# Eleven closing stores of a decode-layer gradient kernel, issued by SyncE instead of GpSimd

## The chip, the cores and the metric

The kernel runs on one core of one Trainium2 chip. A core has five engines with a queue of instructions each: TensorE (PE, with its weight loads as PEld), VectorE (DVE), ScalarE (ACT), GpSimd (POOL) and SyncE (SP, which computes nothing). Data between HBM and the on-chip memory is moved by 16 DMA engines; a transfer is issued by one of the engine queues, and its landing is told by a semaphore. The metric is the device time of one execution in microseconds (us); the times of several executions are given by their median. In the profile, times count from the first instruction, and the span is the time from the first to the last one.

## What is computed

The kernel computes one decode step of a transformer layer (attention over a window of cached keys and values, then a gated feed-forward stage, both with layer norms modulated by a condition vector `c`), and all its gradients for a given `grad_out`. The forward part of the reference, cut to what matters here:

```python
# B = S = 1, D = 1024, 32 query heads, 4 key/value heads, head size 128, cache 65536, window W = 4096
mod = (silu(c) @ w_mod).reshape(1, 6, 1, -1)              # sa, ca, ga, sb, cb, gb
h = layernorm(x) * (1 + ca) + sa
x = x + ga * attention(h, k_cache[..., -W:, :], v_cache[..., -W:, :], wq, wo)
h = layernorm(x) * (1 + cb) + sb
x = x + gb * ((sigmoid(h @ w_gate) * (h @ w_up)) @ w_down)
return x
# outputs: x, and by jax.vjp the gradients of x, k_cache, v_cache, wq, wo, w_gate, w_up, w_down, c, w_mod
```

There is a single token, so every weight gradient is an outer product of two vectors: the row of the gradient of `wq` that belongs to input `j` is `h1[j]` times the gradient of `q`. The gradients of the two caches are zero outside the window (120 MB of zeros in all) and dense in the 4096 positions inside it.

## The kernel before, in words

Only the memory traffic is large: 60.30 MB are read and 185.60 MB written. The schedule is written out by hand: each engine executes its instructions in the order in which the program text records them, and a framework adds the semaphore waits (for data, for buffers that are to be overwritten, and for the DMA semaphores themselves). DMAs issued by GpSimd use eight semaphores in turn, those issued by SyncE and ScalarE eight others; a DMA whose semaphore is still held by an earlier one waits for that one's landing.

GpSimd issues nearly all transfers: the caches, the weights, the zero stores of the cache gradients (`zero`, L160 to L169, placed all over the program so that the DMA engines have work at all times), and nearly all dense results. SyncE issues the first loads of `w_mod`, the loads and stores of `w_down` and its gradient in the feed-forward stage (`load_wd` L852, `store_wd` L855), two late loads (L1120) and three small rows of results (`col_to_row_out`, L251).

The big on-chip buffer is `arena`, cut by hand: `ar(off, size)` is a piece of `size` KB per partition. Buffers are used again as soon as their last use is over. In the closing stage these matter:

- `sec(j)` (L1122) forms columns 2048 to 6143 of the gradient of `w_mod` for block `j` on VectorE, and stores 1 MB from `sec_t[j]`. `sec_t[7]` lies at 56, 8 KB long.
- `dV(g)` and `dK(g)` (through `grad_kv`, L1153) form the dense part of a cache gradient: 32 small matmuls per head, eight evictions `L1162` (ScalarE) or `L206` (VectorE; for dK the two take turns), and one store of 1 MB at L1167, from `kv_home`.
- `dwq_tile(j)` (L1172) is an outer product on VectorE (`outer_dve`, recorded as L206) and a store of 1 MB (L1174), from `dwq_t[j]`.
- `s2(j)` (L1176) forms columns 0 to 2047 of the gradient of `w_mod` on VectorE (also L206) and stores 512 KB (L1178), from `s2_t[j]`. `s2_t[3]` lies at 56, so `s2(3)` has to wait for the landing of `sec(7)`'s store.

The last part of the program is `dK(0)`, `dwq_tile(4)`, `s2(0)`, `s2(1)`, `dK(1)`, and then the eleven steps `dwq_tile(5)`, `s2(2)`, `s2(3)`, `dK(2)`, `dwq_tile(6)`, `s2(4)`, `s2(5)`, `dK(3)`, `dwq_tile(7)`, `s2(6)`, `s2(7)`. At that place all zero stores have been issued. The closing line of the kernel (L1330 in the profile of the kernel before) holds what the framework adds: SyncE waits for every semaphore of the program, each engine executes a DRAIN and reports to GpSimd, GpSimd waits for the other four, clears semaphores and releases them, in two rounds.

Of the kernel before, what the change touches and what calls it, by code (L numbers as in the profile page):

```python
# [19 lines left out]
D = 1024  # L20
# [14 lines left out]
SCALE = DH ** -0.5  # L35
# [23 lines left out]
def kernel(  # L59
# [26 lines left out]
    nc = tc.nc  # L86
# [13 lines left out]
    def ar(off, size):  # L100
        return arena[:, int(off * KIB):int((off + size) * KIB)]
# [79 lines left out]
    def new_ps(name="ps"):  # L181
        p, tag = next_pool()
        return p.tile([P, 512], FP32, name=name, tag=tag)
# [17 lines left out]
    def cp(out, a):  # L201
        return nc.vector.tensor_copy(out=out, in_=a)  # L202

    def ts(out, a, s1, op0, s2=None, op1=None):
        if op1 is None:
            return nc.vector.tensor_scalar(out=out, in0=a, scalar1=s1, scalar2=None, op0=op0)  # L206
        return nc.vector.tensor_scalar(out=out, in0=a, scalar1=s1, scalar2=s2, op0=op0, op1=op1)
# [35 lines left out]
    def outer_dve(out, col, b):  # L243
        return ts(out, b, col, ALU.mult)
# [65 lines left out]
    dwq_view = out_4.rearrange("(j p) n -> p j n", p=P)  # L310
    dwm_view = out_10.rearrange("(j p) n -> p j n", p=P)
# [797 lines left out]
    dS = ar(168, 8)  # L1109
# [3 lines left out]
    kv_home = [ar(o, 8) for o in (184, 64, 72, 80, 96, 104, 112, 120)]  # L1113
    dwq_t = [ar(o, 8) for o in (88, 40, 152, 0, 8, 16, 32, 48)]
    s2_t = [ar(o, 4) for o in (148, 24, 28, 56, 60, 184, 188, 64)]
# [26 lines left out]
    def make_hd(src, name):  # L1142
        tp = new_tp("tp_hd")
        for g in range(G):
            nc.tensor.transpose(tp[32 * g:32 * g + 32, 0:P], src(g), ident_bf[:, :], tile_position=(0, 32 * g))
        hd = late.pop()
        cp(hd, tp[:, 0:P])
        return hd

    def kv_out(og, g):  # L1150
        return og[0, g, SKW:, :].rearrange("(p t) d -> p (t d)", t=KT)

    def grad_kv(rows, hd, og, scale, g, dst, engs):  # L1153
        for tb in range(KT // 4):
            ps = new_ps("ps_kv")
            for t4 in range(4):
                t_ = tb * 4 + t4
                nc.tensor.matmul(ps[:, t4 * DH:(t4 + 1) * DH], lhsT=rows[32 * g:32 * g + HG, t_ * P:(t_ + 1) * P],  # L1158
                                 rhs=hd[32 * g:32 * g + HG, :], start=True, stop=True, tile_position=(32 * g, 0))
            o = dst[:, tb * 512:(tb + 1) * 512]  # L1160
            if engs[tb % len(engs)] == "A":
                nc.scalar.activation(out=o, in_=ps[:, :], func=ACT.Copy, scale=float(scale))  # L1162
            elif scale == 1.0:
                cp(o, ps[:, :])
            else:
                ts(o, ps[:, :], float(scale), ALU.mult)
        nc.gpsimd.dma_start(out=kv_out(og, g), in_=dst)  # L1167

    dV = lambda g, engs: grad_kv(P_b2, DO_hd, out_3, 1.0, g, kv_home[g], engs)
    dK = lambda g, engs: grad_kv(dS, Q_hd, out_2, SCALE, g, kv_home[4 + g], engs)  # L1170

    def dwq_tile(j):  # L1172
        outer_dve(dwq_t[j], h1[:, j:j + 1], dq_b)
        nc.gpsimd.dma_start(out=dwq_view[:, j, :], in_=dwq_t[j])  # L1174

    def s2(j):  # L1176
        outer_dve(s2_t[j], cs_col[:, j:j + 1], dmod_b2)
        nc.gpsimd.dma_start(out=dwm_view[:, j, 0:2 * D], in_=s2_t[j])  # L1178

    zero(Z_END[0])  # L1180
    do_ps = new_ps("do_ps")[:, 0:HQ]
# [32 lines left out]
    Q_hd = make_hd(lambda g: q_col2[:, HG * g:HG * g + 32], "Q_hd")  # L1214
# [36 lines left out]
    dV(0, "A")  # L1251
    sec(4)
    dwq_tile(0)
    dV(1, "A")
    zero(Z_END[3])
    sec(5)
    dwq_tile(1)
    dV(2, "A")
    sec(6)
    dwq_tile(2)  # L1260
    bcast(dmod_bf[:, 0:16], 16, dmod_b2, "A")
    dcs01 = matvec_T(lambda jb, nb: w01_T[:, nb, jb * P:(jb + 1) * P], dh1_hl, "dcs01")
# [24 lines left out]
    dK(0, "AV")  # L1287
    dwq_tile(4)
    s2(0)
    s2(1)  # L1290
    dK(1, "AV")
    dwq_tile(5)
    s2(2)
    s2(3)
    dK(2, "AV")
    dwq_tile(6)
    s2(4)
    s2(5)
    dK(3, "AV")
    dwq_tile(7)  # L1300
    s2(6)
    s2(7)
    keep[0] = 0
    zero(len(zleft))
    assert not zleft and not narrow and not jobs and not bq
# [29 lines left out]
```

## Time and profile before

| | us |
|---|---|
| median of 3 runs | 601.98 |
| lowest and highest of them | 601.69, 602.49 |
| the profiled execution | 600.56 |
| its span | 598.5 |
| busy in it: PE, PEld, DVE | 408.8, 275.9, 336.6 |
| busy in it: ACT, POOL | 266.2, 166.8 |

The span was filled with 412 GB/s on average. How to read what follows: the page cuts the span into 40 equal slices of 15 us and gives for each the mean busy share of the 16 DMA engines in tenths, and what they moved in GB/s. The stretches are the same sums for windows that the reader chooses; a DMA share somewhat above 1 comes from packets that overlap on an engine. The timeline gives each instruction's start, its duration, its engine and line, what it writes and reads, and in brackets how long the engine had been idle before it and what ended that. A GpSimd DMA instruction shows in it only with the time of its issue; its landing is found with the DMA's own line. A line such as "L1330 POOLq DRAIN x3: 46/93/16344" gives the shortest, median and longest duration in ns, and then the first and last start in us.

### The profile page before, as it was taken

The page shows a single profiled execution, that of the slowest core. Times are in us where ns is not written, and L with a number is a line of the kernel's source. Part 1 is how long each engine was busy: PE and PEld are TensorE (multiplying, and loading weights), DVE is VectorE, ACT ScalarE, POOL GpSimd, SP SyncE. Part 2 cuts the span into 40 slices and gives each one's busy share as a digit, 9 for nine tenths or more (in the row PEclk, how much of TensorE's full clock was granted, in tenths as well). Part 3 has the DMA queues.
Part 4 walks back from the last instruction along what each step waited for, and adds up shares of the span by engine and source line. Part 5 has one row for each costly group of instructions (what it writes and reads, how often), then busy time and mean ns, then how long its engine had stood idle before and what let it go on. Part 6 is the DMA issues. An engine that isn't in the chain of part 4 may idle for free.

```text
span 598.5 us, 11039 instructions
## 1 busy us (share of the span) xinstructions
PE 408.8 (68%) x4587; PEld 275.9 (46%) x4612; DVE 336.6 (56%) x641; ACT 266.2 (44%) x408; POOL 166.8 (28%) x264
## 2 busy tenths in 40 slices
PE   3997688999999989999984435544445096765300
PEld 3995334334344545546653434434434066555300
DVE  3653499999511010160007598795796887768530
ACT  2489514567212014213225565673664746873200
POOL 3113123222222212222221233342423363122330
PEclk9999699999999999999995555555555586755555
DMA  8999999999999999999999999999999999999996
GB/s 348 420 417 421 414 427 413 427 423 425 428 419 425 423 427 424 422 424 423 423 397 412 420 387 413 406 398 414 406 404 412 420 422 412 421 424 426 424 416 279
DMA packets 45026, 246.63 MB, mean 412 GB/s; under 512 B 5085, under 2 KB 5085, under 8 KB 24544
## 3 DMA queue, kind: packets, MB, share of 16 engines
q0 software_dynamic: 39120, 225.99, 98.2%
q1 hardware_dynamic: 5808, 19.93, 9.9%
q8 instruction: 36, 0.59, 0.4%
q14 instruction: 14, 0.11, 0.0%
q10 hardware_dynamic: 48, 0.01, 0.0%
HBM read 60.30 MB, written 185.60 MB: 411 GB/s over the span
## 4 chain that ended last, share of the span: by engine, by line
PE 43%; DMA 26%; DVE 17%; ACT 6%; issue 5%; POOL 0%; ACTq 0%; POOLq 0%; SPq 0%; DVEq 0%
PE b_ps L692 17%; DMA out_dram<-arena 15%; DMA arena<-in_B_w_gate_dram 7%; PE n_ps L637 6%; DVE arena L206 4%; DVE arena L193 4%; DVE arena L210 3%; DVE junk L210 3%; PE t_ps L599 2%; DMA arena<-in_B_w_down_dram 2%; PE tp_side L837 2%; ACT arena L838 2%; PE tp_wq L454 2%; PE w_ps L395 2%; PE tp_k L435 1%
## 5 line engine op out<-in xcount | busy, mean ns | idle before, releaser
L692 PE MATMUL b_ps<-arena 128*128 128x512 bf16 x494 | 113.4, 379 | 1.0 <-issue 0.2
L169 POOL DMA_DIRECT2D out_dram<-zeros x114 | 62.3, 548 | 179.7 <-DMA out_dram<-zeros 56.6
L837 PE MATMUL tp_side<-ident_bf,arena 128*128 128x128 bf16 x432 | 51.7, 300 | 48.8 <-ACT arena L838 41.9
L193 DVE TENSOR_TENSOR arena<-arena 128x2048 bf16<-128x2048 bf16 x64 | 76.5, 1223 | 2.3 <-PE n_ps L637 0.3
L692 PEld LDWEIGHTS <-arena 128*128 128x128 bf16 x512 | 48.7, 98 | 55.9 <-issue 2.9
L838 ACT COPY arena<-tp_side 128x1024 bf16<-128x1024 bf16 x54 | 54.0, 1012 | 41.7 <-PE tp_side L837 40.8
L210 DVE CUSTOM_DVE_ANT_0 arena<-arena,scr 128x1024 bf16<-128x1024 bf16 x56 | 66.2, 1220 | 9.8 <-ACT scr L991 9.8
L637 PE MATMUL n_ps<-arena 128*128 128x512 bf16 x249 | 65.1, 378 | 6.9 <-DVE arena L193 5.0
L837 PEld LDWEIGHTS <-arena 128*128 128x128 bf16 x432 | 43.4, 139 | 53.8 <-issue 53.4
L241 ACT ACTIVATE arena<-scr,h 128x1024 bf16<-128x1024 bf16 x35 | 40.1, 1148 | 9.6 <-DVE dh2acc L210 7.8
L637 PEld LDWEIGHTS <-arena 128*128 128x128 bf16 x256 | 24.6, 97 | 41.6 <-issue 16.2
L202 DVE CAST arena<-b_ps 128x512 bf16<-128x512 f32 x6 | 4.1, 691 | 61.6 <-PE b_ps L692 61.6
L1162 ACT ACTIVATE arena<-ps_kv 128x512 bf16<-128x512 f32 x48 | 26.1, 681 | 27.9 <-PE ps_kv L1158 27.5
L210 DVE CUSTOM_DVE_ANT_0 junk<-arena,b1k 128x1024 bf16<-128x1024 bf16 x28 | 34.2, 1222 | 6.1 <-DMA arena<-in_B_w_down_dram 5.7
L601 ACT CAST arena<-t_ps 128x512 bf16<-128x512 f32 x56 | 30.1, 589 | 12.1 <-PE t_ps L599 12.1
L1158 PE MATMUL ps_kv<-junk,arena 8*128 8x128 bf16 x256 | 27.1, 304 | 11.1 <-DVE arena L206 9.8
L869 POOL DMA_DIRECT2D out_dram<-arena x28 | 21.4, 768 | 39.7 <-ACT arena L241 29.8
L1158 PEld LDWEIGHTS <-arena 8*128 8x128 bf16 x256 | 25.2, 141 | 12.9 <-issue 12.9
L456 ACT COPY arena<-tp_wq 128x1024 bf16<-128x1024 bf16 x23 | 21.8, 1032 | 8.6 <-PE tp_wq L454 8.6
L865 POOL DMA_DIRECT2D arena<-in_B_w_up_dram x14 | 10.7, 762 | 51.6 <-DMA out_dram<-arena 29.1
L954 PE MATMUL fg<-h_bf,arena 128*128 128x1 bf16 x448 | 14.7, 166 | 12.5 <-DMA arena<-in_B_w_gate_dram 10.3
L206 DVE TENSOR_SCALAR arena<-arena,cs_col 128x4096 bf16<-128x4096 bf16 (+1 forms) x16 | 16.0, 1018 | 7.5 <-DMA out_dram<-arena 7.5
(302 smaller groups left out, 646.2 us busy)
## 6 DMA issues: line engine op xcount, KB each, us to landing
out_dram<-zeros POOLq DMA_DIRECT2D x114, 1024.0 KB, 15.5
out_dram<-arena POOLq DMA_DIRECT2D x32, 1024.0 KB, 18.3
out_dram<-arena POOLq DMA_DIRECT2D x36, 512.0 KB, 12.7
arena<-in_A_wq_dram POOLq DMA_DIRECT2D x8, 1024.0 KB, 20.6
arena<-in_A_wo_dram POOLq DMA_DIRECT2D x8, 1024.0 KB, 11.8
arena<-in_w_mod_dram POOLq DMA_DIRECT2D x7, 1024.0 KB, 17.8
arena<-in_B_w_down_dram SPq DMA_DIRECT2D x14, 512.0 KB, 9.9
arena<-in_B_w_up_dram POOLq DMA_DIRECT2D x14, 512.0 KB, 9.4
```

The costliest lines, as they stand in the source:

```text
L169: ins = nc.gpsimd.dma_start(out=region.bitcast(FP32), in_=zeros[:, :])
L193: return nc.vector.tensor_tensor(out=out, in0=a, in1=b, op=op)
L206: return nc.vector.tensor_scalar(out=out, in0=a, scalar1=s1, scalar2=None, op0=op0)
L210: return nc.vector.tensor_tensor_reduce(out=out, in0=w, in1=b, scale=1.0, scalar=0.0, op0=ALU.mult, op1=ALU.add, accum_out=acc)
L241: return nc.scalar.activation(out=out, in_=b, func=ACT.Copy, scale=col)
L601: nc.scalar.copy(out=o, in_=ps)
L637: mm = nc.tensor.matmul(nbank[k][:, :], lhsT=k_nat[:, g, t_ * DH:(t_ + 1) * DH], rhs=vp[:, t_ % 2, 4 * k:4 * k + 4, :].rearrange("p h d -> ...
L692: mm = nc.tensor.matmul(bbank[p][k][:, :], lhsT=a4[:, p, h, :], rhs=wo_t[u][:, a, k * 512:(k + 1) * 512], start=(i == 0 and a == 0), stop= ...
L837: nc.tensor.transpose(tp[:, i * P:(i + 1) * P], blk[:, i * P:(i + 1) * P], ident_bf[:, :])
L838: nc.scalar.copy(out=blk if dst is None else dst, in_=tp[:, :])
L1158: nc.tensor.matmul(ps[:, t4 * DH:(t4 + 1) * DH], lhsT=rows[32 * g:32 * g + HG, t_ * P:(t_ + 1) * P], rhs=hd[32 * g:32 * g + HG, :], start= ...
L1162: nc.scalar.activation(out=o, in_=ps[:, :], func=ACT.Copy, scale=float(scale))
```

## The change

The eleven last stores get another issuing queue. `grad_kv`, `dK`, `dwq_tile` and `s2` take the queue as an argument that is GpSimd's by default, and the eleven last steps pass SyncE's. The order of the steps is the same, and so are buffers, sizes and computations. By the built programs, TensorE, VectorE and ScalarE execute the same instructions in the same order as before; GpSimd's list ends with the store of `dK(1)`, and SyncE's list has the eleven stores behind its three small ones. `dK(0)`, `dK(1)`, `dwq_tile(4)`, `s2(0)` and `s2(1)` stay with GpSimd. Line numbers of the closing line shift from L1330 to L1328.

```diff
-    def grad_kv(rows, hd, og, scale, g, dst, engs):
+    def grad_kv(rows, hd, og, scale, g, dst, engs, queue=nc.gpsimd):
...
-        nc.gpsimd.dma_start(out=kv_out(og, g), in_=dst)
+        queue.dma_start(out=kv_out(og, g), in_=dst)
...
-    dK = lambda g, engs: grad_kv(dS, Q_hd, out_2, SCALE, g, kv_home[4 + g], engs)
-
-    def dwq_tile(j):
+    dK = lambda g, engs, queue=nc.gpsimd: grad_kv(dS, Q_hd, out_2, SCALE, g, kv_home[4 + g], engs, queue)
+
+    def dwq_tile(j, queue=nc.gpsimd):
         outer_dve(dwq_t[j], h1[:, j:j + 1], dq_b)
-        nc.gpsimd.dma_start(out=dwq_view[:, j, :], in_=dwq_t[j])
-
-    def s2(j):
+        queue.dma_start(out=dwq_view[:, j, :], in_=dwq_t[j])
+
+    def s2(j, queue=nc.gpsimd):
         outer_dve(s2_t[j], cs_col[:, j:j + 1], dmod_b2)
-        nc.gpsimd.dma_start(out=dwm_view[:, j, 0:2 * D], in_=s2_t[j])
+        queue.dma_start(out=dwm_view[:, j, 0:2 * D], in_=s2_t[j])
...
     dK(1, "AV")
-    dwq_tile(5)
-    s2(2)
-    s2(3)
-    dK(2, "AV")
-    dwq_tile(6)
-    s2(4)
-    s2(5)
-    dK(3, "AV")
-    dwq_tile(7)
-    s2(6)
-    s2(7)
+    tail = nc.sync
+    dwq_tile(5, tail)
+    s2(2, tail)
+    s2(3, tail)
+    for g in (2, 3):
+        dK(g, "AV", tail)
+        dwq_tile(4 + g, tail)
+        s2(2 * g, tail)
+        s2(2 * g + 1, tail)
     keep[0] = 0
```

## The prediction

> **What bounds the kernel now.** I read the page's slices first, then the busy time by stretch of the last 28 us, then the timeline of the tail, then the instructions of the closing line L1330.
>
> ```profile
> span 598.5 us, 11039 instructions
> ...
> DMA  8999999999999999999999999999999999999996
> GB/s 348 420 417 421 414 427 413 427 423 425 428 419 425 423 427 424 422 424 423 423 397 412 420 387 413 406 398 414 406 404 412 420 422 412 421 424 426 424 416 279
> ...
> q0 software_dynamic: 39120, 225.99, 98.2%
> q1 hardware_dynamic: 5808, 19.93, 9.9%
> ```
>
> The DMA engines are full from the second slice to the last but one. GpSimd's DMAs run as q0, SyncE's as q1. The last slice is short of a full one, so what an edit at the end can win lies there.
>
> ```profile
> 570.00:580.00 10.00, 0.00 (x0) 0.00 (x0) 3.96 (x6) 0.00 (x0) 3.57 (x5) 0.50 1.02 417
> 580.00:590.00 10.00, 0.00 (x0) 0.00 (x0) 0.00 (x0) 0.00 (x0) 1.06 (x2) 0.50 1.01 415
> 590.00:598.50 8.50, 0.00 (x0) 0.00 (x0) 0.00 (x0) 0.00 (x0) 0.00 (x0) 0.50 0.42 171
> ```
>
> The columns are length, busy PE, PEld, DVE, ACT, POOL, granted clock, DMA share, GB/s. All arithmetic is done before 574; from there on only transfers run. From 590 the share is 0.42 of 8.5 us: the transfers fade out, then nothing is moved for over 3 us (by single microseconds: 397 GB/s in 591 to 592, 107 in 594 to 595, 0 from 595).
>
> ```profile
> 544.08 0.53 POOL L1126 DMA_DIRECT2D out_dram<-arena  x1 [1.90 <-DVE dct L193]
> ...
> 561.47 0.53 POOL L1174 DMA_DIRECT2D out_dram<-arena  x1 [1.89 <-DMA out_dram<-arena]
> 563.39 0.75 DVE L206 TENSOR_SCALAR arena<-arena,cs_col 128x2048 bf16<-128x2048 bf16 x1 [7.48 <-DMA out_dram<-arena]
> ...
> 581.36 0.53 POOL L1178 DMA_DIRECT2D out_dram<-arena  x1 [0.70 <-DMA out_dram<-arena]
> ```
>
> The eleven stores are those that GpSimd issues from 561.47 (`dwq_tile(5)`) to 581.36 (`s2(7)`). In the timeline it takes one about every 2.45 us per MB, each time after an earlier store has landed: its DMAs use eight semaphores in turn, so it keeps eight in flight. It only tops up a queue that is never empty. VectorE waited until 563.39 for the section store of 544.08 to land, because `s2(3)` overwrites that store's buffer.
>
> ```profile
> L1330 SPq EVENT_SEMAPHORE  x12: 17/28/28, 594.4 to 598.4; - x12
> L1330 POOLq EVENT_SEMAPHORE  x4: 17/17/17, 597.7 to 598.4; - x4
> L1330 POOLq DRAIN  x3: 46/93/16344, 581.3 to 598.2; - x3
> L1330 SPq DRAIN  x3: 7/7/7, 596.2 to 597.9; - x3
> ```
>
> ```profile
> L1178 POOL DMA_DIRECT2D out_dram<-arena x8: 532/532/1517, 553.9 to 581.4; - x8
> ...
> DMA to landing us min/median/max: 14.2/14.4/18.3
> ```
>
> This is what the chain of waits does not show (it ends at the last compute or GpSimd instruction, near 582). The last store, issued at 581.36, lands 14.2 us later, at 595.6. SyncE, which waits for every semaphore, reaches its drains at 596.2. But GpSimd's own DRAIN, begun at 581.3, lasts 16.34 us, to 597.7, which is 2.1 us after the landing. Only then GpSimd collects the engines (its first event at 597.7), and the span ends 0.75 us later.
>
> **What the Trainium skill says.** (1) "DMA: Bandwidth & Descriptors", section "Issuing engines are not separate DMA queues": DMAs of SyncE, ScalarE and GpSimd run on the same 16 engines, and another issuer saves only sequencer time. The trace agrees. In 464 to 474 us, where both queues only store:
>
> ```profile
> DMA packets 767, 4.23 MB, mean 423 GB/s; under 512 B 81, under 2 KB 81, under 8 KB 420
> ## 3 DMA queue, kind: packets, MB, share of 16 engines
> q0 software_dynamic: 484, 3.18, 81.6%
> q1 hardware_dynamic: 282, 1.04, 47.3%
> ```
>
> That is 423 GB/s, no more and no less than q0 alone (417 in 570 to 580). (2) Same page, "Queues, rings and completion order": an engine takes turns between queues packet by packet, and a completion write lands only after the engine's earlier writes across its queues. The trace agrees: in 442 to 446 us q0 moved 0.86 MB and q1 0.77; and q1's four-byte packets, median 9 ns, took 0.36 to 2.18 us in 93 cases of the feed-forward stage. (3) "Perfetto Trace Analysis", "DMA Instruction — SWDGE (GPSIMD)": a GpSimd DMA's recorded end is the end of its descriptors, not of its data. It agrees: 532 ns against a landing after 14.2 us. No page that I found says what GpSimd's DRAIN waits for; that I take from the trace alone.
>
> **The change part by part.** *Bytes*: none change. Dwq 3 x 1 MB, dK 2 x 1 MB, s2 6 x 0.5 MB, 8 MB in all. At the tail's 2.45 us per MB that is 19.6 us of full engines in both kernels. Service per MB, from the queue rows: q0 0.982 x 598.5 x 16 / 225.99 = 41.6 us; q1 0.099 x 598.5 x 16 / 19.93 = 47.6 us, less the 112.7 us of its 93 slow four-byte packets 41.9. Equal within 1%, so rate change 0. Bounds: if q1 cuts 8 KB rows into 4 KB packets (it has carried no row over 4 KB so far), each costs 2 x 159 - 309 = 9 ns more (packet medians of the tail in the DMA records); 5 MB are 640 rows, 40 per engine, 0.36 us. The other end: no gain above 1.5%, since 64 KB per engine in 2.45 us is already 26.8 GB/s on every engine, -0.3 us.
>
> *Issue*: removes eleven GpSimd issues of 0.53 us and adds eleven on SyncE (a 512 KB store of L855 took 0.34 us there): 3.8 us of SyncE, spread over 22 us, hidden behind full DMA queues, so 0. Without that cover it would be 0.34 us once, for the last one. Behind each on SyncE stand only later stores of the same list and the closing waits; ahead of them stand the three small row stores, gone by 545.5. GpSimd has nothing left after dK(1)'s store at about 560 but its DRAIN. The new stores carry waits for older GpSimd landings, too; by the counts in the built program all of those landed long before 555.
>
> *Order*: SyncE doesn't wait for GpSimd's slots. `dwq_tile(5)` is ready at 555.3 and `s2(2)` at 555.9; they were issued at 561.5 and 563.9, and now go at once, taking turns with q0. Their 1.5 MB are served in about 7.3 us at half rate and push q0 back 3.7 us: the section store lands at 563.4 + 3.7 = 567.1. VectorE's `s2(3)` and what is queued behind it (dK(2)'s evictions, hence PE and ACT, up to `s2(7)`) move 3.7 us, ending at 574.0 + 3.7 = 577.7. Who waits? Only SyncE's stores. At 567.1 q0 still holds dwq 3, dK 0, dwq 4, s2 0 and 1, dK 1: 5 MB, 12.2 us, to 579.3, while dK(2)'s store is out at 569.0 + 3.7 = 572.7. The engines stay fed with 6 us in hand (3 for the engines that run 3.6 us ahead): cost 0. If that margin were gone, each us of lateness would cost one.
>
> *End*: the last landing stays at 595.6. SyncE's closing list meets the last semaphore one wait later, leaving one wait of 0.06 us less. GpSimd's DRAIN now follows its own last landing: dK(1)'s store went out at 559.1 and, at 17.3 us for L1167's median, landed at 576.4; with 3.7 to 6 us of q1's bytes served in between, 580 to 582, plus 2.1: by 584.5, off the path. What is late next is SyncE, at 596.2. GpSimd reacts within 0.1 us, as it does in the second round of the closing barrier (598.23 to 598.27). Saved: 597.7 - 596.3 = 1.4, plus 0.06: 1.45 us. Bounds: 0, if SyncE's drains take over the wait; 1.5 at most, because SyncE's 0.6 us of waits remain of the 2.1.
>
> *Sum* against the profiled execution: 598.5 - 1.45 = 597.05 us of span, 600.56 - 1.45 = 599.1 in all (2.06 us lie around the span). That execution was 1.4 us under the median of the three runs; I take the same difference off the median: 601.98 - 1.45 = 600.5 us.
>
> **The rivals.** *The wait moves instead of going (same).* SyncE's DRAINs took 7 ns, but its last DMA had landed long before; with fresh stores of its own one may wait as GpSimd's did, or the 4 KB packets (0.36) and some loss between two queues (1% of 22 us, 0.2) eat part. For it: the tail has never been seen with q1 alone. Against: 423 GB/s in the mixed stretch, and SyncE already waited for all landings. Between 601.0 and 602.2.
>
> *Completion packets hold their engine (slower).* q1's four-byte packets averaged 0.263 us over 388 in 330 to 480 us. If such a packet keeps the engine, not only its queue, eleven stores cost 11 x 0.263 = 2.9 us while no other work covers it: 600.5 + 2.9 = 603.4. It cancels the gain at 0.13 us per store and makes the kernel slower at 0.24. For it: the stretch of the two queues together is some 20 us of the new tail. Against: in 464 to 474 us the shares add to 129% at 423 GB/s, so such packets overlapped with moving data.
>
> *The change does nothing to the end*: GpSimd's DRAIN waits for all DMAs of the core, not its own: 602.0. Against: nothing in the trace separates it, but the 16.3 us began after its own last issue.
>
> **How the numbers follow.** About 0.2%, 1.2 us, is what a measurement can tell from no change, so faster begins at 600.78. Forecast, drain off the path and the last landing within 0.5 us: 0.62, of it 0.50 below 600.78 and 0.12 just above. Wait moved or gain eaten, or the DRAIN unaffected: 0.24. Packets hold the engine: 0.12. A last landing earlier by over 0.5 us: 0.02. So faster 0.52, same 0.36, slower 0.12. The range 599.8 to 602.4 holds the first two cases with both bounds of the rate, and leaves out the slow one.
>
> **What would show it.** GpSimd's long DRAIN ends before 590. Its first event on the closing line comes within 0.1 us of SyncE's first DRAIN, and the span ends 1.4 us after the last landing instead of 2.9. Moved stores start near 555; VectorE's wait before `s2(3)` ends near 567; DMA stays at 410 to 425 GB/s to 590. Wrong if GB/s dips from 582 on, where q1 is alone, if the last landing is past 596.5, or if a SyncE DRAIN grows to 1 us.

## The result and the profile after

The changed kernel takes 599.26 us (median of 6 runs, 598.03 to 600.15); the kernel before, in 6 runs beside it, 601.84 us. The ratio is 0.9957, 95% interval 0.9942 to 0.9972: 2.6 us faster, between 1.7 and 3.5. Measured once more it was 0.9966 (0.9957 to 0.9974), 2.0 us. The forecast of 600.5 us had the direction, the place and the mechanism, but its range began at 599.8 and missed the time.

The profiled execution took 598.03 us with a span of 596.2 (before 600.56 and 598.5). First the closing line of the changed kernel, number, shortest, median and longest duration in ns, first and last start in us:

```profile
L1328 SPq EVENT_SEMAPHORE  x12: 17/28/28, 578.4 to 596.2; - x12
L1328 POOLq EVENT_SEMAPHORE  x4: 17/17/17, 595.5 to 596.1; - x4
L1328 POOLq DRAIN  x3: 46/102/30021, 558.4 to 596.0; - x3
L1328 SPq DRAIN  x3: 7/7/7, 595.4 to 595.7; - x3
```

GpSimd's long DRAIN now begins at 558.4 and is over at 558.4 + 30.0 = 588.4, long before the transfers. SyncE reaches its first DRAIN at 595.4, and GpSimd's first event follows at 595.5. Before, SyncE was there at 596.2 and GpSimd at 597.7. From the last landing to the end of the span it is now 1.34 us (594.91 to 596.25) instead of 2.87 (595.58 to 598.46). This is the predicted step, 1.53 us instead of 1.45.

The issue of dK(1)'s store, the last on GpSimd, by the line L1167 in 558 to 559 us:

```profile
L1167 POOL DMA_DIRECT2D out_dram<-arena x1: 534/534/534, 558.4 to 558.4; - x1
...
DMA to landing us min/median/max: 28.4/28.4/28.4
```

It landed at 558.4 + 28.4 = 586.7 (in the kernel before the same store took 16.8 us to land), and the DRAIN ended 1.65 us after that. The timeline of the tail in the changed kernel:

```profile
554.97 0.36 SPq L1174 DMA_DIRECT2D out_dram<-arena  x1
555.64 11.24 SPq L1178 DMA_DIRECT2D out_dram<-arena  x2
...
558.38 0.53 POOL L1167 DMA_DIRECT2D out_dram<-arena  x1 [1.95 <-DMA out_dram<-arena]
565.76 0.75 DVE L206 TENSOR_SCALAR arena<-arena,cs_col 128x2048 bf16<-128x2048 bf16 x1 [10.20 <-DMA out_dram<-arena]
...
568.98 0.33 SPq L1167 DMA_DIRECT2D out_dram<-arena  x1
```

SyncE issues `dwq_tile(5)` at 554.97, right behind VectorE, instead of at 561.47 from GpSimd; the two stores of the second line are `s2(2)` at 555.64 and `s2(3)`, which ends that row at 566.9. VectorE's wait before `s2(3)` grew from 7.48 to 10.20 us, and nothing came of it, because the transfers had work. The busy time by stretch:

```profile
570.00:580.00 10.00, 0.74 (x7) 0.47 (x5) 6.34 (x10) 0.75 (x2) 0.00 (x0) 0.50 1.01 424
580.00:590.00 10.00, 0.00 (x0) 0.00 (x0) 0.00 (x0) 0.00 (x0) 0.00 (x0) 0.50 1.02 424
590.00:596.20 6.20, 0.00 (x0) 0.00 (x0) 0.00 (x0) 0.00 (x0) 0.00 (x0) 0.50 0.47 193
```

The engines stay at 424 GB/s to 590, also in the second stretch, where SyncE's queue carries 3.36 of 4.24 MB; before it was 417 and 415. The bytes by queue on the page of the changed kernel:

```profile
q0 software_dynamic: 37536, 217.60, 95.1%
q1 hardware_dynamic: 7392, 28.32, 13.1%
```

8.39 MB went from q0 to q1, as the change says.

### The profile page after: what moved, and what is told of

The parts are those of the page before. It is cut to its first block, busy times and chain, and to the rows that moved or that the text cites. A ratio compares the mean times of both kernels' runs of the same rounds, so it can differ in the third digit from the quotient of the medians.

```text
span 596.2 us, 11043 instructions
## 1 busy us (share of the span) xinstructions
PE 409.2 (69%) x4587; PEld 275.6 (46%) x4612; DVE 337.7 (57%) x641; ACT 266.0 (45%) x408; POOL 159.4 (27%) x253
## 4 chain that ended last, share of the span: by engine, by line
DMA 38%; PE 32%; DVE 16%; ACT 5%; issue 4%; POOL 0%; DVEq 0%; ACTq 0%; POOLq 0%; SPq 0%
DMA out_dram<-arena 18%; PE b_ps L692 10%; DMA out_dram<-zeros 9%; PE n_ps L637 6%; DMA arena<-in_B_w_gate_dram 6%; DVE arena L206 5%; DMA arena<-in_B_w_down_dram 4%; DVE arena L193 4%; DVE junk L210 2%; PE t_ps L599 2%; DVE arena L210 2%; PE tp_wq L454 2%; PE w_ps L395 2%; PE tp_side L837 1%; PE tp_k L435 1%
## 5 line engine op out<-in xcount | busy, mean ns | idle before, releaser
L954 PE MATMUL fg<-h_bf,arena 128*128 128x1 bf16 x448 | 14.7, 166 | 11.5 <-DMA arena<-in_B_w_gate_dram 8.7
```

## The experiments

Theory A: GpSimd's DRAIN waits for GpSimd's own last landing, and only its 1.5 us is a steady gain of the change; what was measured beyond it is scatter and something around the span. Theory B: with two queues the transfers themselves end earlier. Theory C: what counts is which queue issues the last store.

**The kernel before again, and the changed kernel again.** No edit to either.

> The kernel before, once more, to learn how much its executions scatter in time, in span and in what lies around the span. Theory A (the 1.45 us of the closing DRAIN is the whole steady gain, and the rest of the measured 2.6 us is scatter and about 0.25 us around the span): ratio within 0.997 to 1.003, spans scattering by more than 1 us, so that the profiled pair's 0.7 us earlier landing lies inside the scatter. Theory B (the transfers themselves end earlier with two queues): scatter of a few tenths only, and the last landing near 595.6.

> The changed kernel once more, on the same chip. Theory A: the time from last landing to the end of the span is 1.35 us again (before 2.9), 1.75 to 1.85 us lie around the span (before 2.06), so the steady gain is 1.5 + 0.25 = 1.75 us, ratio 0.997. Theory B: the ratio is 0.9957 again, 2.6 us, of which 0.7 to 0.9 us is an earlier last landing.

The kernel before against itself: ratio 0.9991 (0.998 to 1.0003). Its executions lie far apart: 51 of them go from 599.96 to 603.59 us. The changed kernel again: 0.9966 (0.9957 to 0.9974), 22 executions from 598.46 to 601.63. In its profiled execution the span was 598.2, as long as that of before, but here too landing to end was 1.34 us; `sec(6)`'s store had landed at 557.4 instead of 555.4, so this execution had come 2 us late into the tail. Before, in its second profile, again took 2.87 us from landing to end. So 1.53 us is steady, and single profiled spans differ by more than that through what happens ahead of the tail. Around the span lie 2.11 us (median; 2.06 to 2.18) in the kernel before and 1.78 (1.73 to 1.84) in the changed one. That 0.33 us is no scatter, and it is followed up below.

**Two stores only, and ten.** The first diff is against the kernel before (only the last two stores are SyncE's), the second against the changed one (the last store goes back to GpSimd).

```diff
     dwq_tile(7)
-    s2(6)
-    s2(7)
+    s2(6, nc.sync)
+    s2(7, nc.sync)
```

> Only the two last stores, s2(6) and s2(7), 1 MB, are SyncE's. Theory A (GpSimd's DRAIN waits for its own last landing plus 2.1 us): the two stores are ready by 574 and overtake, so GpSimd's last store, dwq_tile(7), is pushed back by up to 2.4 us and lands near 595; the DRAIN ends near 597.5 and nearly nothing is gained, 0 to 0.5 us, ratio 0.999 to 1.0. Rival C (what counts is who issues the last store): the whole 1.5 us is gained, ratio 0.9975.

```diff
-        s2(2 * g + 1, tail)
+        s2(2 * g + 1, tail if g == 2 else nc.gpsimd)
```

> Ten stores are SyncE's, the last one, s2(7), stays GpSimd's. Theory A: GpSimd's queue holds only dK(1)'s remainder and this store, so it lands near 589, while SyncE's land to 594.9; the DRAIN ends by 592 and the gain of the whole change is kept, within 0.3 us of it, ratio to before 0.996 to 0.9975. Rival C (who issues the last store) or a DRAIN that waits for all DMAs of the core: the gain of 1.5 us is gone.

This pair decides between A and C. Two stores: 0.9987 (0.9977 to 0.9998), which is 0.8 us, and of that 0.31 us lie around the span. The closing line of this kernel, and then the line of `dwq_tile(7)`'s store, in 580 to 599 us:

```profile
L1330 POOLq EVENT_SEMAPHORE  x4: 17/17/17, 598.8 to 599.4; - x4
L1330 POOLq DRAIN  x3: 46/93/18427, 580.3 to 599.3; - x3
L1330 SPq DRAIN  x3: 7/7/7, 597.3 to 599.0; - x3
```

```profile
L1174 POOL DMA_DIRECT2D out_dram<-arena x1: 534/534/534, 580.3 to 580.3; - x1
...
DMA to landing us min/median/max: 16.4/16.4/16.4
```

SyncE's two stores went ahead and landed at 583.5 and 587.0, in the order of the list the last ones and in time not. GpSimd's `dwq_tile(7)` was pushed back and landed last, at 580.3 + 16.4 = 596.7; the DRAIN ended at 598.75, 2.0 us later, and SyncE had stood ready since 597.3. The wait is there as before: 2.79 us from landing to end. Ten stores: 0.9953 (0.9939 to 0.9968). Its closing line:

```profile
L1328 POOLq EVENT_SEMAPHORE  x4: 17/17/17, 595.6 to 596.2; - x4
L1328 POOLq DRAIN  x3: 46/93/14675, 577.2 to 596.1; - x3
L1328 SPq DRAIN  x3: 7/7/7, 595.5 to 595.8; - x3
```

GpSimd issues the very last store of the list, at 577.2, and yet its DRAIN is over at 577.2 + 14.7 = 591.9, because that store lands at 590.2 while SyncE's land until 595.43. C is refuted from both sides, and so is a DRAIN that waits for all DMAs of the core. And there is something that I had not expected: landing to end is 0.90 us here, not 1.34.

**ScalarE, a shift by one semaphore, sixteen stores, and ten again.** The three diffs are against the changed kernel.

```diff
-    tail = nc.sync
+    tail = nc.scalar
```

> The eleven stores are ScalarE's instead of SyncE's. Theory A (GpSimd's own late landing is the cost, whoever else takes the stores): the closing stretch is 1.35 us again. The store of s2(3), which waits for the section store's landing, now stands ahead of dK(2)'s evictions on ScalarE; with some 6 us of queued transfers in hand that costs nothing, so the ratio to before is 0.996 to 0.998. Rival: SyncE itself matters; then the gain, or the 0.33 us around the span (2.11 before, 1.78 after), is missing here.

```diff
-    col_to_row_out(x2, out_0[0], "x2", late.pop())
+    col_to_row_out(x2, out_0[0], "x2", late.pop(), nc.gpsimd)
```

> The changed kernel with one small row store (2 KB, out_0) given to GpSimd, which shifts SyncE's semaphores by one place, so that the last store's semaphore is the last that SyncE's closing list waits for, and not the third. In the kernel with ten stores the time from last landing to end was 0.87 us against 1.35. Theory A: 0.87 us here too, 0.4 to 0.5 us faster than the changed kernel, ratio to before 0.995 to 0.9965. Rival: the ten-store kernel was faster by scatter or because GpSimd carries a store; then 1.35 us here.

```diff
-    dK(0, "AV")
-    dwq_tile(4)
-    s2(0)
-    s2(1)
-    dK(1, "AV")
     tail = nc.sync
+    dK(0, "AV", tail)
+    dwq_tile(4, tail)
+    s2(0, tail)
+    s2(1, tail)
+    dK(1, "AV", tail)
```

> All sixteen stores from dK(0) on, 12 MB, are SyncE's. Theory A: nothing more is gained than with eleven, because the transfers are bound by the 16 engines; time from the landing of sec(6)'s store to the last landing stays at 39.5 to 39.9 us in all kernels, ratio 0.996 to 0.9975. Theory B (two queues move the tail faster): a larger gain, another 0.3 to 0.5 us.

> The kernel with ten stores on SyncE and s2(7) on GpSimd once more. Theory A: the DRAIN off the path (1.5 us), the last semaphore last in SyncE's list (0.45) and 0.33 us around the span: 2.3 us under before, ratio 0.9955 to 0.997, 0.4 to 0.5 us under the changed kernel.

ScalarE: 0.9963 (0.9951 to 0.9975), landing to end 1.34 us, DRAIN over at 589.1. The taker of the stores doesn't matter, and that ScalarE's evictions stood behind a waiting store cost nothing that shows. Shift by one: 0.9945 (0.9925 to 0.9965), landing to end 0.90 us. Ten again: 0.9959 (0.9944 to 0.9975), 0.91 us. The 0.44 us thus hang on the place of the last store's semaphore in SyncE's closing list: in the changed kernel seven more waits of 0.06 us follow it, in these two none. That is shown by the traces. In the times it is not: the intervals of these kernels and of the changed one overlap.

Sixteen: 0.995 (0.993 to 0.9969), landing to end 1.02 us (two waits follow). Its 0.3 us against the changed kernel's 1.34 come from the shorter list; the times don't resolve more. For theory B the time from the landing of `sec(5)`'s store to the last landing can be compared in all kernels (`sec(6)`'s, which I had named, is itself delayed when sixteen are moved): 46.8 to 47.8 us in six profiles with ten or eleven moved, 47.2 with sixteen, 47.2 and 47.3 in the two of the kernel before. B's 0.7 us, by which the last landings of the first two profiles differ (595.58 and 594.91), isn't there. The times say the same: with landing to end taken off the median span of a kernel, the last landing is estimated at 595.9 to 596.5 with ten or more stores moved, and at 595.7 to 597.0 in the kernel before and all others. But the transfers' rate in the last stretch did change. The stretch of 570 to 590 us, in the kernel before, the changed one, and the one with sixteen:

```profile
570.00:590.00 20.00, 0.00 (x0) 0.00 (x0) 3.96 (x6) 0.00 (x0) 4.63 (x7) 0.50 1.01 416
```

```profile
570.00:590.00 20.00, 0.74 (x7) 0.47 (x5) 6.34 (x10) 0.75 (x2) 0.00 (x0) 0.50 1.02 424
```

```profile
570.00:590.00 20.00, 3.57 (x32) 3.30 (x31) 10.58 (x15) 2.39 (x4) 0.00 (x0) 0.50 1.02 425
```

In the 20 us that end 6 us ahead of the last landing (packets counted by their start), every profile with at most two of the stores moved has 416.6 to 418.6 GB/s, every one with ten or more 423.2 to 425.2. That is 1.6%, 0.3 us in 20; the last landing, which sets the end, does not come earlier by it, and why not is open. Nor is the higher rate a property of a second queue as such. In the kernel before, GpSimd's queue had it nearly alone in 520 to 560 us (16.61 of 16.94 MB), where most rows are of 8 KB:

```profile
DMA packets 2610, 16.94 MB, mean 424 GB/s; under 512 B 323, under 2 KB 323, under 8 KB 705
```

The gap is widest in 575 to 585 us, where rows of 4 and 8 KB follow one another: 409 GB/s before, 422 in the changed kernel. With SyncE taking part in the 4 KB rows near 500 us (one of the kernels below), 500 to 510 us had 413 GB/s, and the kernel before 417 in both profiles. What makes the gap at the end is open.

**What lies around the span.** Four more kernels, each one edit of the kernel before: only `s2(7)` on SyncE; a small row store on GpSimd (the shift's edit, nothing else); the stores of `dwo(0)` and `dwo(1)`, near 500 us, on SyncE; the last two stores on ScalarE.

```diff
-    s2(7)
+    s2(7, nc.sync)
```

> Only s2(7), the last store, is SyncE's. For the DRAIN: it overtakes, GpSimd's s2(6) is pushed to the end and lands last, so landing to end stays near 2.8 us. For the 0.33 us around the span (2.11 us before, 1.78 us with two, ten, eleven or sixteen stores moved): if it goes with the number of GpSimd's instructions or DMAs, one store fewer may leave it at 2.11 or bring 1.8; with a store of another queue at the end, it is 1.8.

> The kernel before with one small row store (2 KB) given by SyncE to GpSimd: one GpSimd DMA more, and nothing at the end changes. If the time around the span goes with the number of GpSimd's or SyncE's instructions, it is 2.11 us or more; if any edit of the program brings 1.78, it is 1.78 here too. Landing to end 2.87.

```diff
-        nc.gpsimd.dma_start(out=wo_dram(out_5, u), in_=wo_t[u])
+        (nc.sync if u < 2 else nc.gpsimd).dma_start(out=wo_dram(out_5, u), in_=wo_t[u])
```

> The kernel before with the stores of dwo(0) and dwo(1), 2 MB near 500 us, on SyncE: two GpSimd DMAs fewer, the tail as before. Around the span: 1.8 us if it goes with the number of GpSimd's DMAs, 2.11 if it goes with the queue of the last stores. Landing to end 2.87 in both theories, so no gain beyond that, ratio 0.999 to 1.0.

> The two last stores are ScalarE's instead of SyncE's. Landing to end 2.8 us as with SyncE, since GpSimd's dwq_tile(7) lands last. Around the span 1.8 us in both theories; 2.11 would tie it to SyncE.

| kernel | ratio to before, 95% interval | landing to end | around the span |
|---|---|---|---|
| before, again | 0.9991 (0.998 to 1.0003) | 2.87 | 2.11 |
| row store on GpSimd | 0.9992 (0.9978 to 1.0005) | 2.92 | 1.77 |
| two in the middle on SyncE | 1.0001 (0.9982 to 1.0021) | 2.80 | 1.79 |
| last one on SyncE | 0.9975 (0.9953 to 0.9996) | 2.84 | 1.78 |
| last two on ScalarE | 0.9991 (0.9974 to 1.0007) | 2.80 | 1.78 |

All times around the span are medians of 10 or more executions that lie within 0.12 us. Each of the edits brings 1.77 to 1.79, the one that gives GpSimd a DMA more as well as those that take one or two away. So the 0.33 us belong to the program of before as it stood, against every other build of it, and not to the queue of the stores. Where in the run they are, the trace can't tell, since it begins with the first instruction; that stays open. (The kernel before is also the only one in which GpSimd issues exactly 256 DMAs; whether that matters, no run shows.) None of the four gets rid of the wait at the end. Three are level with the kernel before; for the last one on SyncE the interval reaches from 0.2 to 2.8 us faster, 0.33 of it explained, and its trace shows no place for more.

**How long the DRAIN outlasts GpSimd's last landing.** The small steps in the column landing to end are no scatter. The traces of all kernels, sorted by the number of DMAs that GpSimd issues in the whole program:

| GpSimd's DMAs | kernels | DRAIN's end after GpSimd's last landing, us |
|---|---|---|
| 240 | sixteen moved | 1.443 |
| 245 | the change (two profiles), the same with ScalarE | 1.648 |
| 246 | ten moved (two profiles), shift by one | 1.688 to 1.689 |
| 254 | last two on SyncE, last two on ScalarE, two in the middle | 2.014 to 2.015 |
| 255 | last one on SyncE | 2.056 |
| 256 | before (two profiles) | 2.097 |
| 257 | row store on GpSimd | 2.137 |

A straight line of 0.041 us per DMA passes within 0.001 us of all seven. Two stores of 512 KB at the end and two of 1 MB in the middle count alike, and a row store of 2 KB counts as one more. So this rest of the wait goes with the number of GpSimd's DMAs, not with their bytes, and not with whether stores of another queue are still under way. Why it does, the traces don't show, and nothing under 240 or over 257 was measured. In the changed kernel it lies off the path; in a kernel in which GpSimd lands last, two DMAs fewer took 0.07 to 0.08 us off the end (2.79 to 2.80 for 2.87).

## Why the prediction was right and wrong

*Right: the end.* "GpSimd's DRAIN now follows its own last landing" is shown by two, ten, eleven, and sixteen moved stores: the DRAIN's end followed GpSimd's landing by 1.4 to 2.1 us each time, wherever that landing was. The 2.1 us that the prediction adds to the landing is no constant, as the table shows; in the changed kernel it was 1.65. Landing to end fell from 2.87 to 1.34, 1.53 us for the predicted 1.45. The rival of a wait that passes on to SyncE is out: its drains kept 7 ns with fresh stores of its own.

*Right: issue and order.* SyncE's issues cost nothing that shows. The section store landed at 565.7 instead of the predicted 567.1, so VectorE's chain was 2.4 us late instead of 3.7, and the margin held. Mis-sized without effect was dK(1)'s landing: 586.7, not 580 to 582. I had let q1's bytes delay it only by those of the first 1.5 MB and a little more; but SyncE's later stores went on taking turns with it: in 570 to 580 us SyncE's queue moved 2.26 MB and GpSimd's 1.97.

*Right: no engine held.* The completion packets of q1 took at most 16 ns in the tails of both profiles of the changed kernel, and its 8 KB rows travel as packets of 8 KB with a median of 309 ns, like q0's. So neither the slow rival's 2.9 us nor the 0.36 us of smaller packets exist.

*Wrong: the sum.* The step that failed is "(2.06 us lie around the span). That execution was 1.4 us under the median of the three runs; I take the same difference off the median", with the range built on it. It carried over two terms that did not stay. The time around the span was 1.78 us instead of 2.11: 0.33 us, which each edit tried brought. And the median of three, 601.98, was 0.30 us above the 601.68 of 51 executions of the same kernel; they spread over 3.6 us, so that medians of three or six runs are uncertain by some tenths, on both sides of the ratio, while the range held only the bounds of the mechanisms. The term of the DRAIN itself was off by 0.08 us (1.53 for 1.45). From 601.68, the 1.53 + 0.33 = 1.86 us lead to 599.8; the second measurement, with the most runs, gave 599.64, 2.0 us (1.6 to 2.6) under before. The first gave 599.26, 2.6 us (1.7 to 3.5); what it has beyond 1.86 lies within its interval, and no profile shows a place for it. With these two terms alone right, the forecast would have been 601.98 - 1.86 = 600.1, which the range still held; what took the result out of it is, as far as the runs show, the scatter, for which it had no room.

*Right for the end, wrong for the rate: "rate change 0".* The last landing did not move, but in the last 20 us the rate rose by 1.6%, a little over the prediction's bound of 1.5%, which it had not worked out from a measured ceiling. Its own lines had the sign of it: 423 GB/s in the mixed stretch is not "no more and no less" than 417, but 1.4% more. And "another issuer saves only sequencer time" holds for the last landing, not for the end of the kernel, which came 1.53 us earlier behind it.

## What to carry to other kernels

At the end of a kernel that is bound by transfers, read the closing instructions as well as the transfers: GpSimd drains its own DMAs, which here took 1.4 to 2.1 us past its last landing, the longer the more DMAs it had issued, and every engine waits for that. Let another queue carry the last stores, enough of them that GpSimd's last one lands some us early (5.2 us were enough here); the order of landing decides and not the order of issue, since a store on an empty queue overtakes a full one. And before a small gain is put down to a mechanism, measure an edit that can't have it: here such an edit changed the time around the span by 0.33 us, against 1.53 of the mechanism.

## What the runs showed of the hardware

- GpSimd's closing DRAIN ended 1.44 us after GpSimd's last landing with 240 GpSimd DMAs in the program and 2.14 us after it with 257, 0.041 us more for each DMA. SyncE's DRAIN took 7 ns in all of them.
- The closing stores of 4 and 8 KB rows ran at 416.6 to 418.6 GB/s with at most two of them off GpSimd's queue, and at 423.2 to 425.2 with ten or more on SyncE's or ScalarE's; mostly 8 KB rows ran at 424 by GpSimd's queue nearly alone (520 to 560 us).
- Each closing wait of SyncE behind the last landed semaphore costs 0.06 us; the place of that semaphore in the list was worth 0.44 us.
- Behind a second queue that takes turns with it, GpSimd's store of dK(1) took 28.4 us to land; in the kernel before the same store took 16.8.
